# Issue order of the first transfers, and the place of a few casts and transposes, in a fused attention and feed-forward kernel

## The chip, the cores and the metric

The kernel runs on one core of a Trainium2 chip. The metric is the device time of one execution in microseconds (us). Quoted times are medians of several executions.

A ratio is the mean time of one kernel's fast runs over that of the other's fast runs in the same rounds on the same chip. So it isn't quite the ratio of the medians. It comes with a 95% interval.

## The reference, cut to what matters

Two layers follow one another: attention in a window of 32 positions to each side, then a feed-forward layer with an ELU between its two matrix products.

```python
# q, k, v: (8, 8, 576, 64) float32   (batch, heads, positions, head size)
scores = q @ k.T / sqrt(64);  scores = where(|i - j| <= 32, scores, -1e9)
attn   = softmax(scores) @ v                     # per batch and head
x      = attn.transpose(0, 2, 1, 3).reshape(4608, 512)
h      = x @ w_in                                # (4608, 2048)
g      = where(h > 0, h, exp(min(h, 0)) - 1)
out    = g @ w_out                               # (4608, 512)
```

## The kernel before: the parts that count here

The bulk of the time is a dense stream of feed-forward steps: eight matmuls of 256 columns with `w_in`, ACT's exponential, two DVE instructions that make `g`, four matmuls of 512 columns with `w_out`. The attention of later batches is threaded through it. Before that stream can begin, the attention of the first positions of batch 0 has to be done with nothing to hide it. That part is called the front here. What it needs:

- q and k of batch 0 in two halves (`HALF_A`, `HALF_B`), loaded by SyncE and ACT as float32, cast to bf16, transposed on TensorE, copied from PSUM into `qT` and `kT`;
- the values, loaded by GpSimd's queue with a cast on the way, in five pieces `load_v(0, m)`, each into the same tile `Ve` (called `V_e` in the program), whose 65th column per head is set to one by a memset;
- the weights in four blocks each, loaded by the same GpSimd queue;
- masks, made by GpSimd.

A `gate` is a load of a single element. It makes SyncE wait until its source is written, and so holds back the loads that SyncE issues after it.

```python
    for which in range(2):
        load_qk(0, which, HALF_A, (nc.sync, nc.scalar))
    zeros = ...; nc.vector.memset(zeros, 0.0)

    def edges(i):
        nc.vector.memset(V_e[i][:, :, :, D:VD], 1.0)          # the ones column
        nc.vector.memset(V_e[i][0:32, 0], 0.0)
        nc.vector.memset(V_e[i][96:128, VS - 1], 0.0)
        if i < 2:
            ...                                               # two memsets on the edges of kT[i]
    edges(0)
    edges(1)
    ident = ...; make_identity(nc, ident)
    masks = ...                                               # GpSimd: memset, two selects
    for m in (1, 0, 2):
        load_v(0, m)
    ...                                                       # GpSimd: three small selects
    gate(masks[0:1, 3, 0:1])
    for which in range(2):
        load_qk(0, which, HALF_B)
    load_w_in(0)
    for m in (3, 4):
        load_v(0, m)
    load_w_out(0)
    load_w_in(1)
    load_w_out(1)
    ...
    idle(8, "y1")                                             # filler matmuls on zeros
    front_cast(0, HALF_A, nc.vector)                          # cast of the first q, on DVE
    front_transpose(0, HALF_A, nc.scalar, ("h0", "h1"))
    ...                                                       # k, scores, exponentials, masks, values
    for i in (0, 1):
        idle(1, "h1")
        x_transpose(i)
        x_evac(i, nc.scalar)                                  # copy of x from PSUM, on ACT
    idle(2, "h1")
    front_cast(0, HALF_B, nc.scalar)
    front_cast(1, HALF_B, nc.vector)
    ...
    at(1, "mid", front_transpose, 1, HALF_B, nc.scalar, ("s", "u"))   # after the second step
    at(1, "mid", front_transpose, 0, HALF_B, nc.vector, ("y0", "y1"))
```

Each engine works through its own instructions in the order of the program. The program builder puts in the waits between engines.

The softmax here doesn't subtract the row's maximum and nothing guards it: scores larger than these inputs give would overflow.

Of the kernel before, what the change touches and what calls it, by code (L numbers as in the profile page):

```python
# [9 lines left out]
FP32 = mybir.dt.float32  # L10
# [5 lines left out]
def _bap(ap, new_ap, off=0):  # L16
    return bass.AP(tensor=ap.tensor, offset=ap.offset + off,
                   ap=[list(x) for x in new_ap])
# [3 lines left out]
def kernel(  # L22
# [9 lines left out]
    nc = tc.nc  # L32
# [61 lines left out]
    def ps_tile(shape, dt, tag, name):  # L94
        return pools[tag].tile(shape, dt, tag=tag, name=name)
# [4 lines left out]
    KPAD = 2 * WIN  # L100
    kT = [cpool.tile([128, KPAD + HP * S + KPAD], BF16, name=f"kT{i}")
          for i in range(2)]
# [9 lines left out]
    WHOLE, HALF_A, HALF_B = (0, SJ), (0, SJ // 2), (1, SJ // 2)  # L112
    qk_f = {}

    def load_qk(b, which, part, engs=(nc.sync, nc.sync)):
        z, nj = part
        t = lpool.tile([128, 2, nj * D], FP32, tag=f"f{which}{nj}",
                       name=f"f{which}")
        qk_f[b, which, z] = t
        src = (q, k)[which][b, :, z * NC * nj:(z + 1) * NC * nj, :].rearrange(  # L120
            "(g h) (c j) d -> c g h (j d)", h=2, j=nj)
        for h in range(2):
            engs[h].dma_start(out=t[:, h, :], in_=src[:, :, h, :])  # L123

    def load_v(b, m):
        lo = 128 * m - WIN
        p0 = max(0, -lo)
        p1 = min(128, S - lo)
        nc.gpsimd.dma_start(  # L129
            out=V_e[b % 3][p0:p1, m, :, 0:D],  # L130
            in_=v[b, :, lo + p0:lo + p1, :].rearrange("h p d -> p h d"))
# [16 lines left out]
    def gate(src, dt=BF16, eng=nc.sync):  # L148
        gates[0] += 1
        t = cpool.tile([1, 1], dt, name=f"gate{gates[0]}")  # L150
        eng.dma_start(out=t, in_=src)

    def load_w_in(c):
        w = D_FF // 4
        nc.gpsimd.dma_start(
            out=w_in_sb[:, :, c * w:(c + 1) * w],
            in_=moe_w_in[:, c * w:(c + 1) * w].rearrange(
                "(o p) f -> p o f", p=128))

    def load_w_out(c):  # L160
        n = NFO // 4
        nc.gpsimd.dma_start(
            out=w_out_sb[:, c * n:(c + 1) * n, :],
            in_=moe_w_out[c * n * 128:(c + 1) * n * 128, :].rearrange(
                "(o p) f -> p o f", p=128))

    def w_in_at(c):
        return w_in_sb[0:1, 0, (c + 1) * (D_FF // 4) - 1:(c + 1) * (D_FF // 4)]
# [7 lines left out]
    def edges(i):  # L176
        nc.vector.memset(V_e[i][:, :, :, D:VD], 1.0)
# [3 lines that stand above are left out]
            for c0, n in ((KPAD - WIN, HP), (KPAD + HP * S, 1)):  # L181
                z = kT[i][:, c0:c0 + WIN]
                nc.vector.memset(_bap(z, [z.ap[0], [S, n], [1, WIN]]), 0.0)

    edges(0)
    edges(1)

    ident = cpool.tile([128, 128], BF16)
    make_identity(nc, ident)



    masks = cpool.tile([128, 5, QB], BF16, name="masks")
# [4 lines left out]
    nc.gpsimd.affine_select(  # L198
        out=masks, in_=masks, compare_op=ALU.is_ge, fill=0.0,
        base=2 * WIN, pattern=[[0, 5], [1, QB]], channel_multiplier=-1)  # L200
    for m in (1, 0, 2):
        load_v(0, m)
    for mi in (0, 4):
        nc.gpsimd.affine_select(
            out=masks[:, mi, :], in_=masks[:, mi, :], compare_op=ALU.is_ge,
# [4 lines left out]
        channel_multiplier=-1)  # L210
    kinds = ["FE", "EE", "EL", "LF"]

    gate(masks[0:1, 3, 0:1])
    for which in range(2):
        load_qk(0, which, HALF_B)
    load_w_in(0)
    for m in (3, 4):
        load_v(0, m)
    load_w_out(0)
    load_w_in(1)  # L220
    load_w_out(1)

# [7 lines left out]
    def copy_on(eng, d_, s_):  # L230
        if eng is nc.scalar:
            nc.scalar.copy(d_, s_)  # L232
        else:
            eng.tensor_copy(d_, s_)  # L234

    def cast_qk(b, which, part, j0, n, eng):
        z, nj = part
        if (b, which, z) not in qk_b:
            qk_b[b, which, z] = lpool.tile(
                [128, nj, 2 * D], BF16, tag=f"b{which}{nj}", name="qkb")  # L240
        t = qk_b[b, which, z]
        copy_on(eng,
                t[:, j0:j0 + n, :].rearrange("p j (h d) -> p h j d", h=2),
                qk_f[b, which, z][:, :, j0 * D:(j0 + n) * D].rearrange(
                    "p h (j d) -> p h j d", d=D))
# [20 lines left out]
    def transpose_qk(b, which, part, j0, n, evac, tag="t0"):  # L266
        z, nj = part
        src = qk_b[b, which, z]
        pt = ps_tile([128, 1024 if n <= 8 else 2048], BF16, tag, "ptx")
        for j in range(n):  # L270
            nc.tensor.transpose(  # L271
                pt[:, j * 128:(j + 1) * 128], src[:, j0 + j, :], ident)
        d = keys_or_queries(b, which)
        copy_on(evac,
                _bap(d, [d.ap[0], [S, HP], [nj, NC], [1, n]],
                     z * NC * nj + j0),
                _bap(pt, [pt.ap[0], [1, HP], [HP, NC], [128, n]]))
# [48 lines left out]
    def normalize(i):  # L326
        psS = st[i][0]
        rc = apool.tile([128, HP, 2], FP32, tag="rc")
        nc.vector.reciprocal(
            rc, _bap(psS, [psS.ap[0], [VD, HP], [512, 2]], D))  # L330
        x_st = apool.tile([128, H, D], BF16, tag="x_st")
        nc.vector.tensor_mul(  # L332
            x_st, _bap(psS, [psS.ap[0], [VD, HP], [512, 2], [1, D]]),
            _bap(rc, [rc.ap[0], [2, HP], [1, 2], [0, D]]))
        st[i][3] = x_st

    def x_transpose(i):
        x_st, tag = st[i][3:]
        pt = ps_tile([128, NDO, 128], BF16, tag, "psXT")
        for do in range(NDO):  # L340
            nc.tensor.transpose(
                pt[:, do, :], x_st[:, 2 * do:2 * do + 2, :], ident)
        st[i] = pt
# [3 lines left out]
    def xT_of(i):  # L347
        t, z = i // 2, i % 2
        if z == 0:
            xT[t] = xpool.tile([128, 2, NDO, 128], BF16, tag="xT", name="xT")  # L350
        return xT[t][:, z, :, :]

    def x_evac(i, eng=nc.vector):
        copy_on(eng, xT_of(i), st.pop(i))
# [12 lines left out]
    def front_cast(which, part, eng):  # L367
        for j0, n in SPLIT:
            cast_qk(0, which, part, j0, n, eng)

    def front_transpose(which, part, evac, tags):
        for (j0, n), tag in zip(SPLIT, tags):
            transpose_qk(0, which, part, j0, n, evac, tag)


    def idle(n, tag):
        ps = ps_tile([128, 512], FP32, tag, "ps_idle")
        for _ in range(n):
            nc.tensor.matmul(ps, lhsT=zeros[:, 0:128], rhs=zeros,
                             start=True, stop=True)  # L380
# [21 lines left out]
    pv(1)  # L402
    for i in (0, 1):
        normalize(i)
    for i in (0, 1):
        idle(1, "h1")
        x_transpose(i)
        x_evac(i, nc.scalar)
    idle(2, "h1")
    front_cast(0, HALF_B, nc.scalar)  # L410
    front_cast(1, HALF_B, nc.vector)


    load_w_in(2)
    load_w_out(2)
    for m in range(3):
        load_v(1, m)
    load_w_in(3)
    load_w_out(3)
    for m in range(3, VS):  # L420
        load_v(1, m)
    gate(w_in_at(1))
    for which in range(2):
        load_qk(1, which, HALF_A)
    gate(w_in_at(3))
# [10 lines left out]
    def at(kk, slot, fn, *args):  # L436
        tasks.setdefault((kk, slot), []).append((fn, args))
# [11 lines left out]
        at(kk + 2, "end", x_evac, i, nc.scalar)  # L449


    at(1, "mid", front_transpose, 1, HALF_B, nc.scalar, ("s", "u"))
    at(1, "mid", front_transpose, 0, HALF_B, nc.vector, ("y0", "y1"))
    at(2, "dve", rotate_v, 0, 2, VS - 1)
    for i, tag in ((2, "s"), (3, "u")):
        at(1, "mid", scores, i, tag)
# [195 lines left out]
```

## Time and profile before

| | before |
|---|---|
| time, median of the first runs | 313.01 us (312.17 to 313.72) |
| span of the profiled run | 309.1 us |
| TensorE busy | 292.7 us, 95% |
| dense stream of matmuls starts | 27.98 us |
| time that TensorE is idle before 28 us | 7.7 us |

The kernel is bound by TensorE. What this change does to the time is decided by the moment at which the dense stream starts:

```profile
27.98 0.71 PE L558 MATMUL ps<-xT,w_in_sb 128*128 128x256 bf16 x5 [0.94 <-ACT xT L232]
```

The front is read in order of time. The prediction below shows its first half. Here is the second half, on ACT and on DVE. A line has the start, the length, the engine and source line, the operation with output and input, and in brackets how long the engine was idle before it and what ended that.

ACT before:

```profile
9.85 1.94 ACT L299 ACTIVATE pu<-psS 128x1024 bf16<-128x1024 f32 x2 [1.19 <-PE psS L288]
13.85 0.58 ACT L232 COPY xT<-psXT 128x512 bf16<-128x512 bf16 x1 [2.06 <-PE psXT L341]
14.68 0.58 ACT L232 COPY xT<-psXT 128x512 bf16<-128x512 bf16 x1 [0.25 <-PE psXT L341]
15.16 1.25 ACT L232 CAST qkb<-f 128x640 bf16<-128x640 f32 x2
```

ACT is idle for 2 us after the exponentials. Only after both copies of x does it cast the second half of q. The change wants to put that cast into the gap.

DVE before:

```profile
17.43 0.83 DVE L234 CAST qkb<-f 128x640 bf16<-128x640 f32 x2 [3.23 <-DMA f<-in_k_dram]
...
22.64 0.69 DVE L308 TENSOR_TENSOR pm<-pu,masks 128x1024 bf16<-128x1024 bf16 x1
23.55 0.69 DVE L308 TENSOR_TENSOR pm<-pu,masks 128x1024 bf16<-128x1024 bf16 x1 [0.22 <-ACT pu L299]
```

DVE waits 3.2 us for the second half of k. The second mask of the second pair of tiles ends at 24.24 us, and 3.74 us later the stream is dense.

### The profile page before, as it was taken

Reading aid. Unit: us, or ns where it says so; the run is one execution under the profiler, and the core shown is the slowest. Engines: PE = TensorE matmul, PEld = TensorE weight load, DVE = VectorE, ACT = ScalarE, POOL = GpSimd, SP = SyncE. Lnnn points to the kernel's source line nnn. Section 1 sums busy time; section 2 is a strip of 40 time slices with the busy share of each in tenths; the row PEclk is TensorE's granted clock in tenths of the full one; section 3 lists DMA queues with packets and bytes.
Section 4 is the critical chain, followed back from the end, with each engine's and each line's share of the span. In section 5 each row is a group of like instructions: output and inputs, shape, how many; then the busy total and the mean of one; then the engine's idle time right before and its main releaser. Section 6 shows DMA issues by size and latency. Waiting matters only on the chain.

```text
span 309.1 us, 7510 instructions
## 1 busy us (share of the span) xinstructions
PE 292.7 (95%) x2996; PEld 197.8 (64%) x3048; DVE 247.0 (80%) x480; ACT 170.6 (55%) x256; POOL 43.8 (14%) x60
## 2 busy tenths in 40 slices
PE   7768999999999999999999999999999999999994
PEld 3446666676666666666766666666666666666662
DVE  6677788899979788888888888888888787876663
ACT  3564756687664674667366736673636363634331
POOL 8733000834101112020202010000000000000000
PEclk9999999999999999999999999999999999999999
DMA  9999999999999999999989999488111111111011
GB/s 191 225 202 233 230 204 383 338 190 241 298 160 180 247 240 196 220 185 317 266 164 143 209 306 193 126 164 171 70 36 68 36 70 35 70 34 70 0 70 69
DMA packets 91657, 52.93 MB, mean 171 GB/s; under 512 B 76518, under 2 KB 80614, under 8 KB 91622
## 3 DMA queue, kind: packets, MB, share of 16 engines
q1 hardware_dynamic: 48022, 36.77, 46.7%
q0 software_dynamic: 41728, 8.92, 37.4%
q10 hardware_dynamic: 1872, 6.75, 6.7%
q8 instruction: 24, 0.39, 0.6%
q14 instruction: 11, 0.09, 0.1%
HBM read 36.70 MB, written 15.34 MB: 168 GB/s over the span
## 4 chain that ended last, share of the span: by engine, by line
PE 82%; DVE 7%; issue 3%; DMA 3%; ACT 2%; POOL 2%; SPq 1%; DVEq 0%; POOLq 0%
PE ps L558 38%; PE psY L592 36%; PE psS L320 3%; PE psS L288 3%; DMA f<-in_k_dram 3%; DVE g_sb L577 2%; DVE pm L308 1%; PE ptx L271 1%; DVE m_sb L567 1%; POOL Ve L129 1%; ACT e_sb L565 1%; DVE x_st L332 1%; ACT pu L299 1%; DVE y_sb L234 1%; SPq L123 1%
## 5 line engine op out<-in xcount | busy, mean ns | idle before, releaser
L565 ACT ACTIVATE e_sb<-ps 128x512 f32<-128x512 f32 (+1 forms) x145 | 86.2, 594 | 119.6 <-PE ps L558 112.8
L558 PE MATMUL ps<-xT,w_in_sb 128*128 128x256 bf16 x1152 | 149.3, 273 | 1.9 <-ACT xT L232 1.2
L592 PE MATMUL psY<-w_out_sb,g_sb 128*128 128x512 bf16 x525 | 139.1, 379 | 3.1 <-issue 0.6
L558 PEld LDWEIGHTS <-w_in_sb 128*128 128x128 bf16 x1152 | 110.7, 98 | 40.4 <-issue 2.2
L577 DVE SCALAR_TENSOR_TENSOR g_sb<-ps,m_sb 128x512 bf16<-128x512 f32 (+1 forms) x145 | 99.5, 686 | 12.9 <-PE ps L558 0.5
L567 DVE TENSOR_SCALAR m_sb<-e_sb 128x512 bf16<-128x512 f32 (+1 forms) x145 | 62.3, 430 | 33.0 <-ACT e_sb L565 30.8
L592 PEld LDWEIGHTS <-g_sb 128*128 128x128 bf16 x576 | 54.5, 98 | 38.3 <-DVE g_sb L577 0.2
L129 POOL DMA_DIRECT2D Ve<-in_v_dram x40 | 34.6, 876 | 131.7 <-PE psS L320 92.5
L299 ACT ACTIVATE pu<-psS 128x1024 bf16<-128x1024 f32 x36 | 36.5, 1020 | 3.5 <-PE psS L288 3.5
L232 ACT CAST qkb<-f 128x768 bf16<-128x768 f32 (+3 forms) x32 | 26.7, 838 | 0.0
L308 DVE TENSOR_TENSOR pm<-pu,masks 128x1024 bf16<-128x1024 bf16 x36 | 24.6, 683 | 1.9 <-ACT pu L299 1.8
L332 DVE TENSOR_TENSOR x_st<-psS,rc 128x512 bf16<-128x512 f32 x36 | 24.9, 692 | 1.2
L320 PEld LDWEIGHTS <-pm 128*64 128x64 bf16 x576 | 11.2, 110 | 10.5 <-DVE pm L308 7.4
L320 PE MATMUL psS<-Ve,pm 128*64 128x65 bf16 x320 | 13.7, 196 | 0.9 <-DVE pm L308 0.8
L140 DVE COPY Vo<-Ve 64x1040 bf16<-64x1040 bf16 x32 | 13.7, 428 | 1.0
L288 PE MATMUL psS<-qT,kT 64*128 64x64 bf16 x576 | 12.2, 193 | 2.4 <-DVE qT L234 1.9
L288 PEld LDWEIGHTS <-kT 64*128 64x128 bf16 x576 | 9.9, 96 | 7.0 <-issue 5.2
L234 DVE COPY y_sb<-psY 128x512 f32<-128x512 f32 x18 | 12.3, 686 | 1.1 <-PE psY L592 0.9
L320 PE MATMUL psS<-Vo,pm 128*64 128x65 bf16 x256 | 12.5, 197 | 0.2 <-DVE pm L308 0.2
L234 DVE CAST qkb<-f 128x1152 bf16<-128x1152 f32 (+3 forms) x14 | 9.2, 679 | 4.0 <-DMA f<-in_k_dram 3.6
L232 ACT COPY y_sb<-psY 128x512 f32<-128x512 f32 x18 | 10.5, 583 | 2.2 <-PE psY L592 2.2
L271 PE MATMUL ptx<-ident,qkb 128*128 128x128 bf16 x108 | 8.9, 235 | 1.7 <-DVE qkb L234 1.7
(32 smaller groups left out, 67.3 us busy)
## 6 DMA issues: line engine op xcount, KB each, us to landing
out_dram<-y_sb SPq DMA_DIRECT2D x35, 256.0 KB, 2.5
f<-in_q_dram SPq DMA_DIRECT2D x12, 576.0 KB, 9.0
f<-in_k_dram SPq DMA_DIRECT2D x12, 576.0 KB, 10.4
in_dram<-qkb ACTq DMA_DIRECT2D x10, 576.0 KB, 8.4
Ve<-in_v_dram POOLq DMA_DIRECT2D x24, 128.0 KB, 11.0
w_in_sb<-in_moe_w_in_dram POOLq DMA_DIRECT2D x4, 512.0 KB, 16.2
w_out_sb<-in_moe_w_out_dram POOLq DMA_DIRECT2D x4, 512.0 KB, 17.1
f<-in_q_dram SPq DMA_DIRECT2D x7, 288.0 KB, 6.3
```

The costliest lines, as they stand in the source:

```text
L129: nc.gpsimd.dma_start(out=V_e[b % 3][p0:p1, m, :, 0:D], in_=v[b, :, lo + p0:lo + p1, :].rearrange("h p d -> p h d"))
L232: nc.scalar.copy(d_, s_)
L288: nc.tensor.matmul(psS[:, h % 2, hp * 128 + z * QB:hp * 128 + (z + 1) * QB], lhsT=kT[b % 2][base:base + 64, KPAD + hp * S + QB * qb - WIN: ...
L299: nc.scalar.activation(pu, _bap(psS, [psS.ap[0], [1, 1024]]), AX.Exp, scale=SCALE)
L308: nc.vector.tensor_mul(pm, pu, _bap(mm, [mm.ap[0], [0, H], [1, 2 * QB]]))
L320: nc.tensor.matmul(psS[QB * z:QB * (z + 1), par, hp * VD:(hp + 1) * VD], lhsT=pm[:, par * HP + hp, z * QB:(z + 1) * QB], rhs=vv[:, qb // 2 ...
L332: nc.vector.tensor_mul(x_st, _bap(psS, [psS.ap[0], [VD, HP], [512, 2], [1, D]]), _bap(rc, [rc.ap[0], [2, HP], [1, 2], [0, D]]))
L558: nc.tensor.matmul(ps[:, j, :], lhsT=w_in_sb[:, do, fo * 128:(fo + 1) * 128], rhs=xT[t][:, :, do, :], start=(do == 0), stop=(do == NDO - 1))
L565: nc.scalar.activation(e_sb, ps, AX.Exp)
L567: nc.vector.tensor_scalar(m_sb, e_sb, -1.0, None, ALU.add)
L577: nc.vector.scalar_tensor_tensor(g_t[kk][:, z * w:(z + 1) * w, :], ps, 0.0, m_t[kk][z], ALU.max, ALU.min)
L592: nc.tensor.matmul(psY[t][ts], lhsT=g_sb[:, j, ts * 128:(ts + 1) * 128], rhs=w_out_sb[:, s * FG + j, :], start=(s == 0 and j == 0), stop=( ...
```

## The change

The change means to issue the first transfers in the order in which they are needed: the values before the masks are made, then the second half of q and k, which is no longer gated on the finished masks but on an early memset, then the weights. The second half then lands early enough to be cast and transposed in the waits of the front. The diff, cut to its core:

```diff
-    edges(0)
-    edges(1)
     ident = ...; make_identity(nc, ident)
+    for m in (1, 0, 2):
+        load_v(0, m)
+    edges(0)
+    gate(kT[0][0:1, KPAD - 1:KPAD])
+    for which in range(2):
+        load_qk(0, which, HALF_B)
+    edges(1)
     masks = ...                       # memset, two selects
-    for m in (1, 0, 2):
-        load_v(0, m)
     ...                               # three small selects
-    gate(masks[0:1, 3, 0:1])
-    for which in range(2):
-        load_qk(0, which, HALF_B)
     load_w_in(0)
+    load_w_out(0)
     for m in (3, 4):
         load_v(0, m)
-    load_w_out(0)
@@
-    for i in (0, 1):
-        idle(1, "h1"); x_transpose(i); x_evac(i, nc.scalar)
-    idle(2, "h1")
     front_cast(0, HALF_B, nc.scalar)
+    idle(1, "h1"); x_transpose(0); x_evac(0, nc.scalar)
+    idle(1, "h1"); x_transpose(1); x_evac(1, nc.scalar)
+    front_transpose(0, HALF_B, nc.scalar, ("y0", "y1"))
     front_cast(1, HALF_B, nc.vector)
@@
-    gate(w_in_at(1))                  # loads of batch 1
+    gate(qk_f[0, 1, 1][0:1, 1, 0:1], FP32)
@@
-    at(1, "mid", front_transpose, 1, HALF_B, nc.scalar, ("s", "u"))
-    at(1, "mid", front_transpose, 0, HALF_B, nc.vector, ("y0", "y1"))
+    at(0, "mid", front_transpose, 1, HALF_B, nc.vector, ("s", "u"))
```

One value load of batch 1 also moves up by one place. No arithmetic is added or taken away, only two filler matmuls go.

More of the change, by code (lines that the diff above doesn't have):

```diff
@@ L404 @@
         normalize(i)
-    for i in (0, 1):
-        idle(1, "h1")
-        x_transpose(i)
-        x_evac(i, nc.scalar)
-    idle(2, "h1")
-    front_cast(0, HALF_B, nc.scalar)
+    front_cast(0, HALF_B, nc.scalar)
+    idle(1, "h1")
+    x_transpose(0)
+    x_evac(0, nc.scalar)
+    idle(1, "h1")
+    x_transpose(1)
+    x_evac(1, nc.scalar)
+    front_transpose(0, HALF_B, nc.scalar, ("y0", "y1"))
     front_cast(1, HALF_B, nc.vector)
     load_w_in(2)
+    load_v(1, 0)
     load_w_out(2)
-    for m in range(3):
+    for m in (1, 2):
         load_v(1, m)
```

## The prediction

> **What bounds the kernel now.** I read the profile in four steps. First the table of stretches (columns: length, then busy time and instruction count of PE, PEld, DVE, ACT, POOL, then granted clock, DMA share and GB/s), to see where TensorE is not busy.
>
> ```profile
> 0.00:10.00 10.00, 7.35 (x60) 3.96 (x60) 6.48 (x18) 3.76 (x6) 9.19 (x20) 1.00 1.09 170
> 10.00:20.00 10.00, 7.33 (x92) 4.48 (x86) 5.50 (x13) 6.64 (x10) 4.13 (x6) 1.00 1.36 242
> 20.00:28.00 8.00, 5.63 (x96) 4.00 (x97) 7.01 (x14) 4.08 (x6) 3.66 (x5) 1.00 1.25 208
> 28.00:40.00 12.00, 11.89 (x104) 8.15 (x105) 8.65 (x17) 6.76 (x9) 0.78 (x1) 1.00 1.42 237
> ...
> 150.00:200.00 50.00, 49.53 (x500) 33.66 (x507) 42.41 (x83) 30.03 (x46) 2.53 (x3) 1.00 1.01 192
> ```
>
> From 28 us on TensorE is full. Its waits after 28 us are for ACT, DVE and issue, under 1 us each, none for a transfer. So the rest of the program can't absorb a late start, and whatever the change does to the moment at which the stream of matmuls becomes dense (27.98 us) goes to the end nearly one to one. Only the first 28 us matter: 7.7 us of them are idle on TensorE, and part of the busy time is filler (matmuls on zeros).
>
> Second, the chain in order of time (start, length, what) shows what sets that moment.
>
> ```profile
> 2.77 2.62 POOL Ve L129 x3
> 5.39 0.78 POOL masks L204 x2
> 6.17 0.21 POOL masks L207
> ...
> 6.39 0.75 SPq L151
> ...
> 9.29 8.12 DMA f<-in_k_dram
> 17.40 0.02 issue
> 17.43 0.83 DVE qkb L234 x2
> ```
>
> The second half of k is issued behind a gate on the masks, at 9.29, and lands at 17.40. DVE had waited 3.2 us for it. That is the wait which the change goes for.
>
> Third, DVE's timeline of the front (start, length, instruction, in brackets the idle time before it).
>
> ```profile
> 0.93 0.27 DVE L174 MEMSET zeros<- 128x256 uint32 x1 [0.93 <-PEq L636]
> 1.30 0.09 DVE L177 MEMSET Ve<- 128x40 bf16 x1
> 1.55 0.49 DVE L178 MEMSET Ve<- 32x520 bf16 x1 [0.16 <-DVE Ve L177]
> 2.19 0.49 DVE L179 MEMSET Ve<- 32x520 bf16 x1
> 2.74 0.14 DVE L183 MEMSET kT<- 128x64 uint32 x2
> ...
> 4.41 0.13 DVE L183 MEMSET kT<- 128x64 uint32 x2
> 4.91 1.17 DVE L234 CAST qkb<-f 128x640 bf16<-128x640 f32 x2 [0.37 <-DMA f<-in_q_dram]
> 6.44 1.02 DVE L234 CAST qkb<-f 128x640 bf16<-128x640 f32 x2 [0.36 <-DMA f<-in_k_dram]
> ```
>
> The edge memsets run from 1.30 to 4.54, free of charge, while the first q and k are in flight. Each cast starts as its load lands, 4.91 and 6.44.
>
> Fourth, the issues of the first three value loads one at a time: started at 2.72, 3.73 and 4.50, to landing 5.1, 4.8 and 4.8 us, so landed at 7.8, 8.5 and 9.3. That is harmless before: the first reader is DVE's rotation at 9.08.
>
> **What the Trainium skill says.** (1) "DMA: Bandwidth & Descriptors", section "Queues, rings and completion order": each DMA engine takes turns between the queues it has work for, packet by packet. The trace agrees where both have small backlogs: from 13.4 to 14.4 us the software queue moved 161 packets and the hardware queue of SyncE 151. It agrees less elsewhere: the second half of q, issued from 7.20, got no data packet until about 11.4, when the first 512 packets of weights were through. (2) The same page, "Anatomy of one DMA — SWDGE (gpsimd) path": about 2 us of a small transfer are fixed, most of it waiting for the last write's receipt. Here the last value packet moved at about 8.35 and the landing was 9.3, so about 1 us of that kind; the first moved at about 5.65, 2.9 us after the first issue began. (3) "TensorE: Matmul & The Clock Gate", "Part 1: The HAM clock gate (the "warmup" mystery)": TensorE starts at half rate and needs about 3.4 us of activity. The trace agrees: a filler matmul took 634 ns until 8.1 us, 390 ns from 10.07.
>
> **The change part by part.**
>
> *Values ahead of the masks.* GpSimd drops 1.32 to 2.78 (one memset, two selects) from ahead of the value issues, so they begin at about 1.37 instead of 2.72. The data gains far less: all 16 DMA engines are busy from about 3 to 8.35 us with the first q and k (394 to 403 GB/s) and then with the values (1,199 packets of 128 bytes in the us from 6.4). The work is the same, so the last packet still moves near 8.3, and I keep the landing at **9.25**. The masks are done near 6.5, needed after 10.9: free.
>
> *Edges behind the values: the hidden cost.* In the new order of the program the three value loads come before the memsets of the same buffer. The built instructions of the changed kernel show it: DVE's second instruction, the memset of Ve's ones column, now waits for all three value loads, although the bytes don't overlap. So after the zeros DVE stands still from 1.2 to 9.25. Then come all its memsets (4.54 - 1.30 = 3.24 us), ahead of the cast of the first q: that starts at 9.25 + 3.24 + 0.05 = 12.55 instead of 4.91, **+7.6**. The first k has long landed, so its 0.36 us of waiting goes: **+7.3** for all that hangs on it (scores, exponentials, masks, values, normalizing, the first x). The copy of the second x from PSUM starts at 14.68 + 7.3 = 22.0, and the first step of the large matmuls at 15.32 + 7.3 = 22.6.
>
> *Second half of q and k behind a gate on kT's edge.* That memset is 1.5 us into DVE's list, so the gate opens at about 10.8 and not at 6.39: these loads are issued 4.4 us later, not earlier. Old landings plus 4.4 give 21.8 for k; counting from when the weights ahead in the DMA engines are through gives about 20. DVE has come to the cast of k at 14.19 + 7.3 = 21.5. So the 3.2 us wait vanishes, but because everything else is late.
>
> *Casts and transposes moved up.* ACT casts q (1.25 us) in its former idle 11.79 to 13.85, which holds it. PE transposes q before and k after the first step. What remains, start to start with the old durations, after the copy of the second x begins: that copy 0.48, q's copy 1.26, exponential 0.65, m_sb 0.34, k's copy 1.34, g_sb 0.69, m_sb 0.45, g_sb 0.70, rotation 0.90, first mask 0.75, second mask 0.65: 8.2 us. In the old run the same two points lie 24.24 - 14.68 = 9.56 us apart. So the rearrangement gives back **1.3**, and hands the bound from the k transfer to DVE's queue.
>
> *The rest* (first weights before values 3 and 4, batch 1 loads gated on k, one value load earlier): the weights of step 2 landed at 24.3 and will be needed near 31; TensorE after 28 us waited for no transfer. I count zero.
>
> Sum: +7.6 - 0.36 - 1.3 = **+6.0 us**, 313.0 to 319.0, which is 1.9%.
>
> **The rivals.**
>
> A. *The intended gain*: the gate opens at 3 us, the second half lands before 13, and the front closes up. With the k wait of 3.2 us gone and the shorter tail, 2 to 4 us would go: 309 to 311. For it speaks that this wait is on the chain. Against it: the memset's wait for the loads is in the built program, and the gate hangs on DVE behind it.
>
> B. *The values land much earlier*, with their issue (9.3 - 1.35 = 7.95): then all is 1.3 us less bad, +4.7, 317.7. Against it: the DMA engines are already full in that time. In a weaker form (0.5 us) it is quite possible.
>
> C. *The second half becomes the bound again*: landing at 21.8 or later instead of 20, or q too late for ACT's gap near 19 us. In-order ACT would then hold up the copies of x: another 0.5 to 1.5 us, 319.5 to 320.5.
>
> D. *TensorE starts cold*: it stands idle from 4.85 to about 13.2, so the eight filler matmuls warm nothing. But the old run became warm only at 10 us, 4.3 us after its first real transpose; I count 0 to 0.5.
>
> E. *DVE frees itself faster*: with fewer collisions the conversions run nearer 0.83 us a pair (as at 17.43) than 1.17: up to 0.5 less.
>
> **Range and chances.** The bulk is one number, DVE's stall, known to some 0.5 us; the give-back of 1.3 is the least sure term (0.3 to 1.8); A is a small chance only. I give 319.0, and 316.8 to 321.0 to hold it 8 times in 10. The 2% line is 319.3, just above my middle: slower 0.45, same 0.53, faster 0.02.
>
> **What would show it.** Right, if DVE's first edge memset shows about 8 us of idle before it with a value load as releaser; if the cast of q starts at 12 to 13; if the gate is issued at 10 to 11.5; if the first large matmul starts at 22 to 23 and the dense stream at 33.5 to 34.5; if TensorE after that looks as before. The landing is wrong if the memset starts before 8.5 or after 10. The give-back is wrong if the second mask ends more than 9 us after the copy of the second x starts. All of it is wrong if DVE's memsets run from 1.3 us as before.

## The result, and the profile after

| | before | after |
|---|---|---|
| time, median of 4 runs | 312.73 us (312.17 to 313.72) | 317.58 us (316.92 to 318.08) |
| ratio to before | | 1.015 (1.0117 to 1.0183) |
| span of the profiled run | 309.1 us | 315.8 us |
| start of the second copy of x | 14.68 us | 23.12 us |
| end of the second mask | 24.24 us | 31.29 us |
| dense stream starts | 27.98 us | 35.03 us |

The changed kernel is 1.5% slower. Line numbers have shifted by a few in it, so L236 is the copy or cast on DVE that was L234.

The stretches after (columns as in the prediction):

```profile
0.00:10.00 10.00, 3.59 (x8) 1.03 (x8) 0.27 (x1) 1.49 (x2) 6.77 (x17) 1.00 1.14 183
10.00:20.00 10.00, 5.27 (x55) 3.31 (x56) 6.86 (x18) 3.82 (x5) 7.42 (x9) 1.00 1.34 212
20.00:28.00 8.00, 6.57 (x111) 4.47 (x112) 5.95 (x13) 5.10 (x10) 1.55 (x2) 1.00 1.29 234
```

In the first 10 us DVE did a single instruction of 0.27 us where it had done 18 for 6.48 us, and TensorE did only its eight fillers. The dense stream on TensorE after:

```profile
35.03 0.71 PE L562 MATMUL ps<-xT,w_in_sb 128*128 128x256 bf16 x5 [0.94 <-DVE m_sb L571]
```

DVE after:

```profile
0.93 0.27 DVE L174 MEMSET zeros<- 128x256 uint32 x1 [0.93 <-PEq L640]
10.15 0.09 DVE L177 MEMSET Ve<- 128x40 bf16 x1 [8.95 <-DMA Ve<-in_v_dram]
...
13.32 0.68 DVE L236 CAST qkb<-f 128x640 bf16<-128x640 f32 x1
...
24.15 1.02 DVE L236 CAST qkb<-f 128x640 bf16<-128x640 f32 x2 [1.53 <-DMA f<-in_k_dram]
25.47 0.43 DVE L571 TENSOR_SCALAR m_sb<-e_sb 128x512 bf16<-128x512 f32 x1 [0.30 <-ACT e_sb L569]
...
30.00 1.29 DVE L310 TENSOR_TENSOR pm<-pu,masks 128x1024 bf16<-128x1024 bf16 x2
```

The second line is the core of it: 8.95 us of idle time before a memset of 0.09 us, ended by a value load. The cast of the first q comes at 13.32 and not at 4.91, although that q had landed long before. The cast of the second half of k still waits for its load, 1.53 us, but the next instruction waits 0.30 us for ACT after it, so that wait no longer sets anything.

The wait between memset and loads also holds GpSimd. The loads of values 3 and 4 write the same tile and stand behind that memset in the program; before, it was long done when they were issued (7.23 us). Now they wait 2.75 us for it, and GpSimd's later loads queue behind them:

```profile
10.54 1.65 POOL L129 DMA_DIRECT2D Ve<-in_v_dram  x2 [2.75 <-DVE Ve L177]
```

ACT after:

```profile
21.25 1.25 ACT L234 CAST qkb<-f 128x640 bf16<-128x640 f32 x2 [1.03 <-DMA f<-in_q_dram]
22.40 1.30 ACT L234 COPY xT<-psXT 128x512 bf16<-128x512 bf16 x2
```

The moved cast of q sits in the gap as intended and even waits for its load there. The copies of x follow at once. The first is late by about 0.1 us through it; the second starts 0.44 us after its transposes, as before (0.43), so it isn't late.

The chain of waits after (start, length, what) says the same from the end of the program backwards:

```profile
1.50 1.77 POOL Ve L129 x2
3.27 6.57 DMA Ve<-in_v_dram
...
10.15 0.10 DVE Ve L177
```

It used to run through the load of the second half of k, and it now runs through the value load and DVE's memsets.

**Values issued earlier didn't land earlier.** They were issued from 1.50 us, not from 2.72, but landed at 8.4, 9.4 and 9.9 us, against 7.8, 8.5 and 9.3 before. The DMA queues from 6 to 7 us (packets, MB, share of 16 engines), after:

```profile
q0 software_dynamic: 582, 0.07, 114.4%
q10 hardware_dynamic: 87, 0.17, 49.0%
```

The same us before:

```profile
q0 software_dynamic: 1227, 0.16, 243.3%
q10 hardware_dynamic: 1, 0.00, 0.1%
```

Before, the first q and k (q1, q10) were through by then and the values (q0) had the engines to themselves. After, ACT's part of the first k (q10) was still in flight beside them: half as many value packets moved in that us, and that part of k landed 6.3 us after its issue instead of 4.9. This shows sharing, but not why the landing is later than 9.3. In the run with the stall alone below, the values were issued at 2.72 as before and moved 1,170 packets from 6 to 7 us, and they landed at 9.9 too. In three profiles of kernels with the changed order of loads and the stall the landing lay at 9.5, 9.8 and 10.0, read from the chain. The cause of these tenths stays open.

### The profile page after: what moved, and what is told of

The parts are those of the page before. It is cut to its first block, busy times and chain, and to the rows that moved or that the text cites. A ratio compares the mean times of both kernels' runs of the same rounds, so it can differ in the third digit from the quotient of the medians.

```text
span 315.8 us, 7506 instructions
## 1 busy us (share of the span) xinstructions
PE 293.0 (93%) x2994; PEld 197.3 (62%) x3046; DVE 246.7 (78%) x480; ACT 170.4 (54%) x256; POOL 43.3 (14%) x60
## 4 chain that ended last, share of the span: by engine, by line
PE 83%; DVE 9%; ACT 2%; issue 2%; DMA 2%; POOL 1%; DVEq 0%; POOLq 0%
PE ps L562 38%; PE psY L596 36%; PE psS L322 3%; PE psS L290 3%; PE ptx L273 2%; DMA Ve<-in_v_dram 2%; DVE g_sb L581 2%; DVE pm L310 1%; DVE x_st L334 1%; DVE m_sb L571 1%; ACT pu L301 1%; ACT e_sb L569 1%; DVE Vo L140 1%; PE psXT L343 1%; DVE kT L236 1%
## 5 line engine op out<-in xcount | busy, mean ns | idle before, releaser
L581 DVE SCALAR_TENSOR_TENSOR g_sb<-ps,m_sb 128x512 bf16<-128x512 f32 (+1 forms) x145 | 99.4, 686 | 12.9 <-PE ps L562 0.5
L571 DVE TENSOR_SCALAR m_sb<-e_sb 128x512 bf16<-128x512 f32 (+1 forms) x145 | 62.3, 430 | 33.5 <-ACT e_sb L569 31.4
L234 ACT CAST qkb<-f 128x768 bf16<-128x768 f32 (+3 forms) x32 | 26.7, 837 | 1.0 <-DMA f<-in_q_dram 1.0
L322 PEld LDWEIGHTS <-pm 128*64 128x64 bf16 x576 | 11.1, 110 | 10.8 <-DVE pm L310 7.7
L273 PEld LDWEIGHTS <-qkb 128*128 128x128 bf16 x108 | 7.4, 105 | 11.7 <-DVE qkb L236 10.9
L234 ACT COPY qT<-ptx 128x1152 bf16<-128x1152 bf16 (+2 forms) x8 | 7.5, 974 | 11.0 <-PE ptx L273 10.9
L236 DVE COPY y_sb<-psY 128x512 f32<-128x512 f32 x18 | 12.3, 686 | 1.2 <-PE psY L596 1.1
```

What stands on the lines that cost most here:

```text
L234: nc.scalar.copy(d_, s_)
L322: nc.tensor.matmul(psS[QB * z:QB * (z + 1), par, hp * VD:(hp + 1) * VD], lhsT=pm[:, par * HP + hp, z * QB:(z + 1) * QB], rhs=vv[:, qb // 2 ...
L571: nc.vector.tensor_scalar(m_sb, e_sb, -1.0, None, ALU.add)
L581: nc.vector.scalar_tensor_tensor(g_t[kk][:, z * w:(z + 1) * w, :], ps, 0.0, m_t[kk][z], ALU.max, ALU.min)
```

## The experiments

Two theories. **S**, the stall: the memsets of `edges(0)` now follow the value loads in the program, DVE waits for these loads, and all else is a consequence. **O**, the order: the new order of the transfers itself costs (crowding, the later second half, weights ahead of values 3 and 4), with or without the stall. In a third question, the move of the casts and transposes is priced by itself.

### The kernel before, again

No edit.

> The kernel before, unchanged, for its own spread: its profiled run (310.8 us) was below all its timed runs (312.2 to 313.7). Both theories: ratio 0.997 to 1.003. Looked at for this: where the dense stream of matmuls starts (27.98 us in the first profile). If it starts at 29 to 30 here, the front of the old kernel varies by itself and the profiles' difference of 6.7 us overstates the change's cost; if at 28 again, the spread is elsewhere.

312.05 us (310.54 to 314.18, 4 runs), ratio 1.0025 (0.9966 to 1.0084). The profiled run was again a quick one, 310.54 us at a granted clock of 1.000, its dense stream at 27.95 us. So neither of the two profiles shows the typical run of this kernel. Over all calls its fast runs go from 310.5 to 314.9 us. The two at a clock of 1.000 took 310.50 and 310.54; the three at 0.981 or 0.982 took 314.55 to 314.86, and the slow one at 0.983 took 315.23. In between the order is loose: runs at 0.995 to 0.997 took from 310.96 to 312.98, and one at 0.991 took 310.81.

### Edges first: the stall undone

```diff
+    edges(0)
     for m in (1, 0, 2):
         load_v(0, m)
-    edges(0)
     gate(kT[0][0:1, KPAD - 1:KPAD])
```

> The changed kernel with one thing undone: the edge memsets of batch 0 stand ahead of the three value loads again. Theory S (the stall of DVE behind the value loads is the whole loss): DVE's memsets run from 1.3 us, the gate opens at about 3 us, the first q is cast at 5 to 6, the dense stream starts at 27 to 29.5 us, time 311 to 314, ratio 0.995 to 1.005. Rival O (the new order of the transfers itself costs, with or without the stall): 316 or more, ratio above 1.01. Side question: values and second half now run side by side, so I expect the values to land at 10.5 to 12 us and DVE's rotation to wait for them.

312.19 us (311.70 to 312.86), ratio 1.0026 (0.9989 to 1.0063). With the rest of the change in place, the loss is gone. That speaks for S and against O. But the intended gain isn't there either. DVE in this run:

```profile
4.92 1.31 DVE L236 CAST qkb<-f 128x640 bf16<-128x640 f32 x2 [0.38 <-DMA f<-in_q_dram]
...
10.88 0.42 DVE L140 COPY Vo<-Ve 64x1040 bf16<-64x1040 bf16 x1 [1.24 <-DMA Ve<-in_v_dram]
...
14.37 0.82 DVE L236 CAST qkb<-f 128x640 bf16<-128x640 f32 x2
...
23.20 0.88 DVE L140 COPY Vo<-Ve 64x1040 bf16<-64x1040 bf16 x2 [2.16 <-DMA Ve<-in_v_dram]
```

The first q is cast at 4.92 again, and the second half of k is cast at 14.37 with no wait, 3 us sooner than before. In its place stand two new waits for values: 1.24 us for the third piece, which shared the engines with the second half, and 2.16 us for pieces 3 and 4. These had been put behind a second block of weights and landed at 23.2 us. TensorE stood idle for 2.73 us meanwhile, and after that its granted clock fell. Its stretches (same columns):

```profile
23.00:24.00 1.00, 0.00 (x0) 0.00 (x0) 0.77 (x2) 0.00 (x0) 0.54 (x1) 1.00 1.22 201
...
27.00:28.00 1.00, 1.00 (x9) 0.82 (x7) 0.46 (x2) 0.93 (x2) 0.00 (x0) 0.50 1.24 207
28.00:29.00 1.00, 1.00 (x7) 0.69 (x6) 0.81 (x2) 0.14 (x1) 0.66 (x1) 0.50 1.24 201
```

The granted clock (third number from the right) is 0.50 just where the real matmuls come. The dense stream started at 30.32 us in this profile, later than the 27 to 29.5 expected.

### The stall alone in the kernel before

```diff
-    edges(0)
-    edges(1)
     ...
     for m in (1, 0, 2):
         load_v(0, m)
+    edges(0)
+    edges(1)
```

> The kernel before with only this changed: all edge memsets stand behind the first three value loads in the program; order of the transfers, gate, casts and transposes as before. Theory S: DVE idle to about 9.5 us, first q cast at 12.5 to 13, second half of k landed long before its cast, dense stream at 34 to 35.5 us, 318 to 320 us, ratio 1.017 to 1.023. Rival O: transfers are as before, so 312 to 314.

317.48 us (317.22 to 317.87), ratio 1.0191 (1.0152 to 1.0231). A kernel with the old loads, gates, casts and transposes is as slow as the changed one as soon as its edge memsets stand behind the value loads. DVE in this run:

```profile
10.18 0.09 DVE L177 MEMSET Ve<- 128x40 bf16 x1 [8.98 <-DMA Ve<-in_v_dram]
...
22.59 0.82 DVE L236 CAST qkb<-f 128x640 bf16<-128x640 f32 x2
...
30.88 0.69 DVE L310 TENSOR_TENSOR pm<-pu,masks 128x1024 bf16<-128x1024 bf16 x1 [0.22 <-ACT pu L301]
```

The second half of k is cast at 22.59 with no wait, and the dense stream starts at 35.32. The time is just under the expected 318. S holds: the stall is sufficient, and the run with edges first showed that it is necessary.

### One instruction moved

Of the memsets of batch 0 only the one of the ones column goes ahead of the loads.

```diff
+    nc.vector.memset(V_e[0][:, :, :, D:VD], 1.0)
     for m in (1, 0, 2):
         load_v(0, m)
-    edges(0)
+    ...                               # the other four memsets of edges(0)
```

> The changed kernel with one instruction moved: the memset of the ones column (0.09 us) ahead of the value loads; the other four memsets of batch 0 stay behind them. The build shows no wait for the loads on any of them then. Theory S: the whole stall hangs on this one instruction's false overlap, so as with all edges first: DVE's memsets from 1.3 us, 311.5 to 313, ratio 0.995 to 1.005. If more of the order matters: 315 or more.

312.75 us (311.84 to 313.31), ratio 0.9986 (0.9937 to 1.0034). None of the memsets waits for a load any more:

```profile
1.30 0.09 DVE L190 MEMSET Ve<- 128x40 bf16 x1
1.55 0.49 DVE L193 MEMSET Ve<- 32x520 bf16 x1 [0.16 <-DVE Ve L190]
```

The order now costs the other side a little: the first value load waits 0.33 us for that memset. So the whole loss hangs on one instruction of 0.09 us. Its column lies between the loaded columns of every head, 65 apart, and touches none of their bytes. The builder still puts the wait in. That it compares the range from first to last element, not the elements, is my reading of it and is not shown. The zero memsets of partitions 0 to 31 and 96 to 127, which lie in no range of these three loads, get no wait.

This run also prices the fallen clock. Its program differs from the one with edges first only in the place of four memsets, and its profile is a near twin: the second mask of the second pair ends at 25.40 us in both, after TensorE had stood idle for 2.60 us (there 2.73). But here the granted clock stayed at 1.00:

```profile
27.00:28.00 1.00, 1.00 (x14) 0.91 (x12) 0.42 (x2) 0.90 (x2) 0.00 (x0) 1.00 1.24 207
```

The dense stream started at 29.32 and not at 30.32, and the profiled runs took 311.84 and 312.86 us. Eight matmuls with `w_in` just before took 1.04 us here and 1.92 there. So a clock at half in that place cost 1.0 us, and an idle stretch of this length doesn't always bring it about.

### The casts and transposes not moved

The changed kernel with its second and fourth blocks of the diff undone: `front_cast`, `front_transpose` and `idle` of the second half back in their old places.

> The changed kernel with the casts and transposes of the second half put back to where they were. If the move gives back 1.3 us as I predicted: second mask ends about 1.3 us later against the copy of the second x, 318.5 to 319.5 us, ratio 1.018 to 1.023. If the move is worth nothing: 317 to 318, as the changed kernel. If it gives back 2 us or more: 319.5 to 320.5.

317.35 us (317.28 to 317.94), ratio 1.0194 (1.0161 to 1.0228). In the profile the second copy of x starts at 23.27 and the second mask ends at 31.68: 8.41 us, against 8.17 with the move. So the move is worth about 0.2 us between these marks, and not 1.3. The dense stream started at 35.42 against 35.03. Two more profiles say the same: 8.41 us in the run with the stall alone, which has no move either, and 8.25 in the second profile of the changed kernel.

### The changed kernel, again

No edit.

> The changed kernel again, so that it shares its runs of the kernel before with the others here. The stall alone gave 1.019 in the last call and the changed kernel without the move of the casts also 1.019; the changed kernel gave 1.015 in another call. If the move gives back 1.3 us as predicted, this shows 1.015 again; if only the tenths that the two profiles show (dense stream at 35.03 against 35.42), 1.017 to 1.019.

317.88 us (317.30 to 318.46), ratio 1.0176 (1.0129 to 1.0222). The intervals of the changed kernel (1.015 and 1.0176) and of the two kernels without the move (1.0191, 1.0194) overlap. The times alone don't resolve the move. In this run's profile the clock had fallen:

```profile
10.00:15.00 5.00, 1.29 (x10) 1.01 (x11) 4.28 (x13) 0.54 (x1) 4.81 (x6) 0.50 1.41 181
15.00:20.00 5.00, 4.14 (x58) 2.45 (x59) 2.95 (x6) 3.51 (x5) 3.41 (x5) 0.63 1.31 258
```

It had fallen within the stall and just after, where TensorE mostly waits for others. The dense stream started at 34.77, no later than in the profile at full clock (35.03), and the run took 317.30 us, no more than the changed kernel's other runs.

### The move alone

The kernel before with only the casts and transposes moved.

> The kernel before with only the casts and transposes of the second half moved; edges, values and the gate on the masks as before. ACT works in order, and the second half of q lands at about 15 us, so the cast now stands ahead of the copies of x (due at 13.8 and 14.7) and holds them: first large matmul at 17 to 17.6 us instead of 15.3, second mask ends 8.2 to 8.4 us after the copy of the second x starts, so dense stream at 28.5 to 29, time 0.5 to 1 us above the kernel before, ratio 1.001 to 1.005. Were the move worth its predicted 1.3 us by itself: 0.996.

312.65 us (312.52 to 312.78), ratio 1.0002 (0.9964 to 1.0040). ACT in this run:

```profile
15.33 1.25 ACT L232 CAST qkb<-f 128x640 bf16<-128x640 f32 x2 [3.57 <-DMA f<-in_q_dram]
```

The expected mechanism is there. The cast stands first in ACT's order, waits 3.57 us for its load, and holds up the copies of x: they start at 16.48, and were due at 13.85 and 14.68. The dense stream started at 30.13 us, later than I had expected (28.5 to 29); in this run the second half of k also landed at 18.4, a us later than before, and TensorE's clock stood between 0.82 and 0.87 for 15 us. The median is that of the kernel before (312.25 in this call). That isn't a contradiction: the profiled run took 312.69 us, 1.9 to 2.2 above the two profiled runs of the kernel before, and its stream started 2.2 us after theirs.

### Old load orders back

On top of edges first:

```diff
     load_w_in(0)
-    load_w_out(0)
     for m in (3, 4):
         load_v(0, m)
+    load_w_out(0)
@@
-    gate(qk_f[0, 1, 1][0:1, 1, 0:1], FP32)
+    gate(w_in_at(1))
```

> Edges ahead of the values as in the run that undid the stall, and in addition values 3 and 4 ahead of the second block of weights again and batch 1 loads gated on the weights of steps 2 and 3 again. In the run with edges first, DVE waited 2.2 us for values 3 and 4, landed at 23.2. Theory S with this new wait: they land at 17 to 20 now, the wait goes, but the weights that follow land at 21 to 22 and those of steps 2 and 3 at 23.5 to 24.5, so the dense stream starts at 26.5 to 28, 310 to 311.5 us, ratio 0.995 to 1.0. If the intended gain of 2 to 4 us were there once nothing stands in its way: 308 to 309.

311.77 us (310.49 to 312.06, 6 runs), ratio 0.9968 (0.9935 to 1.0001). Values 3 and 4 landed at 17 to 18 us and DVE no longer waits for them. But the third piece of the values landed at 12.9 us here, behind the second half of q and k, and the rotation waited 3.6 us for values in two parts, at 10.69 and 12.94. The dense stream started at 29.52, not at 26.5 to 28, and the median is above the 310 to 311.5 that I had expected.

### The second half gated on the first q

On top of that:

```diff
-    gate(kT[0][0:1, KPAD - 1:KPAD])
+    gate(qk_f[0, 0, 0][0:1, 0, 0:1], FP32)
```

> As the run before it, but the second half of q and k is gated on the landing of the first q (about 4.9 us) and not on a memset at 2.9 us, so that the values come ahead of it in the DMA engines. Values landed at 9.5 to 10.3 instead of 10.9, second half at 12.5 to 14, still ahead of its casts or within 0.5 us. Dense stream within 0.5 us of the run before it, either way; ratio 0.995 to 1.0.

310.94 us (309.60 to 312.11, 6 runs), ratio 0.9946 (0.9909 to 0.9984). The second half is now issued from 5.05 us and not from 3.7, and the values came through ahead of it: DVE's rotation had no wait for them, and both casts of the second half still had none. In this profile the first k was late (cast at 7.50), and the dense stream started at 28.02, 1.5 us before that of the run above, where I had expected 0.5 at most.

### Fillers, to keep the clock up

Five more matmuls on zeros in TensorE's gap before the scores of pairs 2 and 3, first in the kernel before, then in the version just above.

```diff
+    at(1, "mid", idle, 5, "s")        # "y0" in the second kernel, where that PSUM tile is free
     for i, tag in ((2, "s"), (3, "u")):
         at(1, "mid", scores, i, tag)
```

> The kernel before with five more filler matmuls on zeros in TensorE's gap before the scores of pairs 2 and 3 (old trace: idle 19.2 to 21.1 us). The old kernel's runs spread from 310.5 to 315.2 us, the low ones at a granted clock of 1.000, the high ones at 0.981 to 0.99; its two profiles both caught a run at 1.000, which is why the profiles differ by more (6.7 us) than the times (4.9 to 5.6). If that spread comes from TensorE's clock falling to half in the sparse front, the fillers help: median 310.6 to 311.5, spread under 2 us. If it comes from elsewhere (transfers): median 312 to 312.5 and the same spread.

In the kernel before: 312.22 us (311.06 to 313.29, 6 runs) against 313.14 (310.96 to 314.86) without them, ratio 0.9965 (0.9927 to 1.0003). The granted clocks rose to between 0.993 and 1.000, from 0.982 to 0.997. The spread shrank to 2.2 us (six runs against eleven), but missed the 2 that I had set, as the median missed its 311.5, and the interval includes 1. The clock can't be all of the old kernel's spread: at a clock of 1.000 two of these runs took 311.06 and 313.09. Another part is the landings: in the profile of this run, at a clock of 0.997, the second q landed at 16.4 us, more than a us late, and the first block of `w_in` held TensorE for 1.6 us.

> The same five fillers in the version with edges first, old load orders and the gate on the first q (310.9 us median, 309.6 to 312.1). If the clock's fall explains its spread: 309.5 to 310.5, ratio 0.990 to 0.994. If not, as without them, 0.9946.

In the other version: 309.63 us (median of the five fast runs, 308.90 to 310.65; with the slow one of 314.65 it is 309.94), ratio 0.9886 (0.9847 to 0.9924). This is 1.1% faster than the kernel before. Its dense stream, on TensorE:

```profile
26.00 1.03 PE L563 MATMUL ps<-xT,w_in_sb 128*128 128x256 bf16 x8 [0.94 <-ACT xT L234]
```

2.0 us sooner than before, at a clock of 1.000 as the profile before. What now stands in front of it is a transfer once more. DVE casts the second k at 13.40 without a wait, and TensorE waits 0.87 us for the first block of `w_out`. How much of the step from 0.9946 to 0.9886 the fillers made can't be said, since the intervals overlap. Of the 2.0 us between their two profiles, 1.0 is the first k, cast at 6.47 here and at 7.50 there.

## Why the prediction was right, point by point

The time lay at 317.58 us, in the range of 316.8 to 321.0. The mechanism, DVE's stall behind the value loads, was read right before any run. The terms were not all of their right size.

| step of the prediction | predicted | profile after |
|---|---|---|
| values landed | 9.25 us | 9.9, DVE goes on at 10.15 |
| memsets before the first cast | 3.24 us | 3.17 |
| cast of the first q | 12.55 us, +7.6 | 13.32, +8.4 |
| gate opens | 10.8 us | 11.73 |
| second copy of x starts | 22.0 us, +7.3 | 23.12, +8.4 |
| that copy to the end of the second mask | 8.2 us, was 9.56 | 8.17 |
| end of the second mask | +6.0 us | +7.05 |
| dense stream | 33.5 to 34.5 us | 35.03 |
| time | 319.0 us, +6.0 | 317.58, +4.85 |

**The stall** was right, and shown from both sides: undone, the loss goes (1.0026); alone in the old kernel, it makes the whole loss (1.0191).

**The landing of the values** was the term mis-sized on the path. DVE went on 0.9 us later than predicted: 0.6 are the landing (9.84 by the chain), and 0.3 the time from the landing to the memset's start, for which the prediction had nothing. I had let the values gain nothing from their earlier issue; they lost, and why is open, as said above. Rival B, that they would land earlier, went the wrong way.

**The rearrangement's 1.3 us** was right as a sum and wrong as an attribution. 8.2 us from the copy of x to the second mask is what the run showed, nearly to the tenth. But the old 9.56 us contained the wait for the second half of k, and that wait goes through the stall itself, without any move: 8.41 us with nothing moved. The move gave about 0.2 us. I had taken the vanished wait to be the move's gift.

**Rival C** occurred in part: ACT waited 1.03 us for q, DVE 1.53 us for k. The last load of k landed at about 24.1 us, not at 20 or 21.8: the gate opened 0.9 us later than predicted, and that load took 9.7 us from issue to landing instead of 8.1. Neither wait cost more than about 0.1 us, because DVE's next instruction waited for ACT anyway.

**Rival D**, the cold start, showed in the durations but not in the sum. In the run of the changed kernel that was profiled a second time the clock was at half from 10 to 15 us, where TensorE had little to do.

**Two readings** in the prediction's part on the skill are off. The second half of q got its first data packets at about 11.5 us, when about 430 of the 512 weight packets had moved, not all. And the trace agrees that fillers are slow first and fast later, but not plainly with 3.4 us: after eight fillers without a break from 1.26 to 4.85, those at 6.70 and 8.09 still took 630 ns, while the profile gives the granted clock as 1.00.

**From the profile to the time.** By the profiles the change cost 6.7 us of span, by the first call's medians 4.85, by the second's 5.6 (312.25 against 317.88). The reason is on the other side of the subtraction. The profile before is of a run at full clock. The kernel before at a clock of 1.000 took 310.50, 310.54 and (the first profile) 310.77 us, and the changed kernel at 1.000 took 317.54: 6.8 to 7.0 us apart, as the profiles have it. But most runs of the kernel before aren't like that, with a median of 312 to 313 us. The changed kernel hardly varies, 316.9 to 318.5 us in eight runs with clocks from 0.981 to 1.000. The 13 profiled runs of all kernels here agree in one thing: the time of the run less the start of its dense stream is 282.5 to 283.2 us, at any granted clock (before 282.79, after 282.51). So what separates these runs happens in the front, and a run of the kernel before of 312.7 us would have started its stream near 30 us; this is an estimate from these numbers, no such run was profiled. I had added a difference read off one quick profile to a median of slower runs. So my landing of 9.25, which was too early, and this, which adds too much, took each other back. That is luck. That the clock's fall makes the old kernel's slow runs is not shown: it cost 1.0 us in one pair of profiles of other kernels, and the fillers raised the clock, but the 0.9 us by which they lowered the median are not clear of no gain at all.

**Where the intended gain went.** With the stall undone, the 3.2 us wait for the second half of k is gone, and the time is that of the kernel before. The gain was spent on new waits for values that the same reordering pushed back. With the value orders restored and the second half let in behind the first q, 0.5% came out of the idea; with fillers 1.1%.

## What to carry to other kernels

Moving a load up past a memset of the same tile turns a write that was free into a wait for the load, even where their bytes don't overlap; read the waits in the built program on every engine's first instructions, above all on an engine whose queue then holds the critical work. When transfers share engines that are already full, an earlier issue of one can delay another, as it did the first k here (6.3 us instead of 4.9), so ask what each reorder pushes back. And before adding a difference of two profiles to a median, see which of the runs the profile caught.

## What the Trainium skill lacked or had wrong

- "DMA: Bandwidth & Descriptors", section "Queues, rings and completion order": the page says that an engine drains a whole packet, of several descriptors, from one queue before it turns to the next. The trace shows sharing (582 value packets in a us beside 87 of the first k, against 1,227 alone), but what it counts as a packet is 128 bytes of a value, so the turns themselves aren't tested. The page doesn't prepare one for a load that waits for most of another queue's block: the second half of q, issued from 7.19 us, got its first data packets only past 11.2 us, with most of the 512 packets of the first block of weights through (5 packets from 11.2 to 11.4 us in the second profile of the kernel before).
- The same page, "Anatomy of one DMA — SWDGE (gpsimd) path": about 2 us fixed and then a rate by bytes, which for 128 KB gives an estimate of 2.3 us, doesn't fit these value loads of 128-byte pieces behind other traffic. One of 128 KB took 4.8 to 5.2 us from issue to landing in the two profiles of the kernel before and 6.6 to 6.9 in the first of the changed one. That small pieces are slow the page does say elsewhere; its fit has no term for them or for traffic.
- "TensorE: Matmul & The Clock Gate", "Part 1: The HAM clock gate (the "warmup" mystery)": a clock at half after an idle stretch is seen (0.50 in the front in two profiles shown here), but after nearly the same stretch it also stayed at 1.00. The page says the ramp penalty can be left out as under 1% of a typical span. No run here contradicts that: the one pair of profiles that prices the fall has 1.0 us of 312.
- No page says how a strided memset and loads into the same tile are ordered against each other, which was the cause of the loss here: 8.95 us of wait before 0.09 us of work.
